# Query masking moved from GpSimd to VectorE, and the branch over a fallback program placed ahead of the last stores with prefetch hints

## The chip, the cores and the metric

The kernel runs on one core of one Trainium2 chip. The core has a matrix engine (TensorE, PE), a vector engine (VectorE, DVE), an activation engine (ScalarE, ACT), a general engine (GpSimd, POOL) and an engine that here only issues DMA transfers (SyncE, SP). They run their own instruction streams and wait for each other through semaphores. The metric is the device time of one launch in microseconds (us); lower is better.

## The reference

The input x has 2048 rows of 512 numbers in bfloat16. It is normalised once, and two branches read the result: an attention block with 32 heads of only 16 dimensions, and a gated feed-forward block of width 1792. Both are added to x.

```python
def _A_ref(x, wqkv, wo):          # H = 32, Dh = 16
    q, k, v = ...                 # (x @ wqkv) split in heads
    scores = jnp.einsum("bhqd,bhkd->bhqk", q, k) * (Dh ** -0.5)
    p = _softmax(scores, axis=-1)
    o = jnp.einsum("bhqk,bhkd->bhqd", p, v)
    return ... @ wo
def _B_ref(x, w1, w3, w2):
    h = _silu(x @ w1) * (x @ w3)
    return h @ w2
xn = _layernorm(x, axis=-1)
return x + _A_ref(xn, A_wqkv, A_wo) + _B_ref(xn, B_w1, B_w3, B_w2)
```

The exponentials are the bulk: 32 heads x 2048 x 2048 scores.

## The kernel before

**Units and chunks.** The attention is cut into 32 units. A unit is one block of 512 queries with four heads, which share the 128 partitions in four groups of 32 rows; each group of 32 holds two heads of 16 dimensions, and an even and an odd unit use one and the other of them. So the same projected queries serve two units (u0 and u0 + 1), once with the rows of the odd heads set to zero and once with the rows of the even heads set to zero. This is what the two masks `msk[:, 0:1]` and `msk[:, 1:2]` do. The tile `QT` has four slots of 128 x 512 for it. A chunk is a pair of score matmuls (L1794, two banks of PSUM, 128 x 1024 numbers); there are 1024 chunks, 32 for each unit, and three PSUM buffers for them.

**Two ways to an exponential.** A chunk goes either to ACT, which takes the exponential in one instruction (L1857, tile `PT`), or to DVE, which builds it from integer arithmetic: a first pass out of PSUM (`p1`, L1930) for each chunk, and then for every two chunks the four passes `m` (L1972), `g` (L1988), `t` (L1979) and `e` (L1994) within SBUF (tile `xd`). PE multiplies either result with the values (L2048).

**The planner.** The order of all instructions on all engines is made by a planner (`_Sched`), when the kernel is built. It plays the work through with a cost for each kind of instruction and gives every chunk to ACT or DVE as they come free; the rest of the work (projections, the feed-forward block, output projections) is put in between when its due position is reached or when PE has room. The due position is counted in score matmuls already issued (64 for a unit). What is on the chip is then a fixed order for each engine, with semaphore waits where data cross from one engine to another.

**The query projection.** `tile_QT(qc, i)` computes one block of projected queries for the unit pair u0, u0 + 1: sixteen matmuls on PE (L1331, with `wq`), then DVE takes the block out of PSUM with a scale (L1462) into slot s1. Then GpSimd makes the two masked copies in four instructions of 128 x 256 (L1470), each posted to start beside a `p1` of DVE (`beside_p1`, and the extra dependence on `st["p1_op"]`). There are 15 such tiles; the first pair of units gets its queries in another way. A tile is due 100 score matmuls before the first score that needs it (L1707). GpSimd's other recurring work is the product L2107 (`onorm`, two halves for each unit pair), which also starts beside a `p1`.

**The end.** After the last unit, PE, ACT and DVE finish four output tiles. They are stored by two DMA transfers of 256 KB that SP issues (L1636). The arithmetic on DVE is exact enough only within limits. DVE therefore checks these limits and writes a word `flag` (L2245); if it is set, a second, slower program (`_plan_max`) must run instead. `run` puts it on every engine: first the whole fast program, then a wait for the flag, a load of it into a register (L2304), and an `If` with the whole slow program inside (L2305 to L2313), which on these inputs is jumped over. SP then waits for its transfers (`emit_end`, L142), and all engines meet in a final barrier (L2316).

## Time and profile before

| what | us |
|---|---|
| time, median of 3 runs | 791.72 |
| lowest and highest of these runs | 790.52 and 792.25 |
| the profiled execution, its own time | 792.25 |
| its span in the trace | 790.5 |
| busy: ACT | 768.5 |
| busy: DVE | 763.5 |
| busy: PE | 747.2 |
| busy: POOL | 90.4 |
| ACT exponentials (L1857) | 796, busy 745.1 |
| DVE first passes `p1` (L1930) | 228, busy 277.2 |

A row of the profile gives line, engine, operation, the tile written and the tile read, the shapes, the count, and then the busy time with the mean duration of one instruction in nanoseconds. Consecutive instructions of an engine overlap a little in the records, so that the step from one start to the next is shorter than the duration: in an unbroken stretch of 90 exponentials it is 0.918 us where the mean duration is 1.161 us, and the passes L1972 and L1988 that follow each other at 35.82, 36.43 and 37.03 us step by 0.60 us where one lasts 0.685 us.

The own time of the profiled execution is 1.75 us more than its span: that part lies outside the first and the last recorded instruction.

### The profile page before, as it was taken

The numbers are of one execution on the slowest core, as the hardware profiler recorded it, in microseconds if no ns is written. First come the engines' busy times: TensorE is split into PE (matmuls) and PEld (weight loads), VectorE is DVE, ScalarE is ACT, GpSimd is POOL, SyncE is SP. The second block draws the span as 40 slices with busy tenths as digits, with TensorE's granted clock in tenths as the row PEclk, the third lists the DMA queues.
The fourth block names the chain that finished last, engine by engine and source line by source line (L and its number), as shares of the span: only waits on it lengthen the run. The fifth ranks groups of instructions, "written<-read, shape, count | busy, mean of one in ns | idle before, by whom it ended". The sixth has DMA issues, their size and how long they took to land.

```text
span 790.5 us, 21316 instructions
## 1 busy us (share of the span) xinstructions
PE 747.2 (95%) x9177; PEld 223.6 (28%) x9177; DVE 763.5 (97%) x1015; ACT 768.5 (97%) x870; POOL 90.4 (11%) x120
## 2 busy tenths in 40 slices
PE   8999999899999999989999999999899999999987
PEld 6422222222222222222222222222222222222223
DVE  8899999999999999999999999999999999999992
ACT  6999999999999999999999999999999999999993
POOL 3200012002020010302102020110201001020000
PEclk9999999999999999999999999999999999999998
DMA  7023122322232232333321134332122343132221
GB/s 214 2 23 114 9 36 29 49 30 32 52 41 22 36 38 36 46 47 49 50 14 33 25 56 49 49 42 28 37 22 22 62 56 37 35 48 16 29 14 34
DMA packets 83440, 32.92 MB, mean 42 GB/s; under 512 B 72072, under 2 KB 79496, under 8 KB 83336
## 3 DMA queue, kind: packets, MB, share of 16 engines
q1 hardware_dynamic: 83336, 31.46, 28.0%
q8 instruction: 74, 1.21, 0.6%
q14 instruction: 30, 0.25, 0.1%
HBM read 22.81 MB, written 2.10 MB: 32 GB/s over the span
## 4 chain that ended last, share of the span: by engine, by line
ACT 80%; PE 11%; DVE 8%; issue 1%; DMA 0%; POOL 0%; DVEq 0%; ACTq 0%
ACT f_PT L1857 76%; PE ps L1331 4%; PE ps L1794 3%; ACT f_th L1554 3%; DVE f_xd L1930 3%; PE ps L2048 2%; DVE f_xd L1979 1%; DVE f_xd L1994 1%; DVE f_xd L1988 1%; DVE f_xd L1972 1%; DVE f_hT L1568 0%; DVE f_t L1558 0%; DMA f_xd<-in_A_x_dram 0%; PE ps L1343 0%; DVE f_stats L1255 0%
## 5 line engine op out<-in xcount | busy, mean ns | idle before, releaser
L1857 ACT ACTIVATE f_PT<-ps 128x1024 bf16<-128x1024 f32 x796 | 745.1, 1161 | 3.8 <-PE ps L1794 3.6
L1794 PE MATMUL ps<-f_QT,f_KT 32*128 32x512 bf16 x2048 | 314.0, 385 | 25.1 <-ACT f_PT L1857 19.0
L1930 DVE TENSOR_SCALAR f_xd<-ps 128x1024 int16<-128x1024 f32 x228 | 277.2, 1216 | 2.3 <-PE ps L1794 1.8
L2048 PE MATMUL ps<-f_PT,f_Vaug 128*17 128x512 bf16 (+1 forms) x1592 | 202.8, 384 | 1.1 <-DVE f_U L2066 0.5
L2048 PE MATMUL ps<-f_xd,f_Vaug 128*32 128x512 bf16 (+1 forms) x1368 | 179.0, 384 | 5.5 <-DVE f_U L2066 3.8
L1794 PEld LDWEIGHTS ps<-f_QT,f_KT 32*128 32x128 bf16 x2048 | 80.2, 91 | 325.8 <-ACT f_PT L1857 265.2
L1331 PE MATMUL ps<-f_xnT,f_w 128*32 128x512 bf16 x1792 | 142.2, 384 | 3.7 <-DVE f_t L1558 1.8
L1979 DVE TENSOR_TENSOR f_xd<-f_xd 128x2048 bf16<-128x2048 bf16 x114 | 139.3, 1222 | 0.0
L1470 POOL TENSOR_SCALAR f_QT<-f_QT,f_msk 128x256 bf16<-128x256 bf16 x60 | 55.4, 923 | 271.7 <-DVE f_xd L1988 112.3
L1972 DVE TENSOR_SCALAR f_xd<-f_xd 128x2048 int16<-128x2048 int16 x114 | 78.0, 684 | 2.7 <-PE ps L2048 2.0
L1988 DVE TENSOR_SCALAR f_xd<-f_xd 128x2048 int16<-128x2048 int16 x114 | 78.1, 685 | 0.0
L1994 DVE TENSOR_SCALAR f_xd<-f_xd 128x2048 int16<-128x2048 int16 x114 | 78.1, 685 | 0.0
L1331 PE MATMUL ps<-f_w,f_hT 128*32 128x512 bf16 x896 | 72.6, 383 | 0.2 <-DVE f_xn_sb L1624 0.2
L2107 POOL TENSOR_TENSOR f_onorm<-f_U,f_R 128x256 bf16<-128x256 f32 x30 | 25.1, 845 | 371.8 <-DMA f_R<-f_Rrow 186.4
L2048 PEld LDWEIGHTS ps<-f_PT,f_Vaug 128*17 128x17 bf16 (+1 forms) x1592 | 49.4, 92 | 59.0 <-issue 45.0
L2048 PEld LDWEIGHTS ps<-f_xd,f_Vaug 128*32 128x32 bf16 (+1 forms) x1368 | 44.1, 92 | 48.9 <-issue 27.8
L1331 PEld LDWEIGHTS ps<-f_xnT,f_w 128*32 128x32 bf16 x1792 | 36.4, 94 | 64.5 <-issue 55.6
L1554 ACT ACTIVATE f_th<-ps 128x512 f32<-128x512 f32 x56 | 41.1, 733 | 0.0
L1568 DVE SCALAR_TENSOR_TENSOR f_hT<-f_t,ps 128x512 bf16<-128x512 bf16 x56 | 37.9, 677 | 0.3
L1558 DVE SCALAR_TENSOR_TENSOR f_t<-f_th,ps 128x512 bf16<-128x512 f32 x56 | 37.9, 677 | 0.2
L1331 PEld LDWEIGHTS ps<-f_w,f_hT 128*32 128x32 bf16 x896 | 19.4, 95 | 23.9 <-issue 16.8
L1331 PE MATMUL ps<-f_wo,f_onorm 128*32 128x512 bf16 x272 | 21.8, 408 | 0.2 <-DVE f_wkv L1613 0.2
(81 smaller groups left out, 244.2 us busy)
## 6 DMA issues: line engine op xcount, KB each, us to landing
f_w<-in_B_w_dram SPq DMA_DIRECT2D x112, 128.0 KB
f_R<-f_Rrow SPq DMA_DIRECT2D x124, 32.0 KB
f_xr<-in_A_x_dram SPq DMA_DIRECT2D x16, 128.0 KB
f_U<-f_U SPq DMA_DIRECT2D x60, 32.0 KB
f_w<-in_B_w_dram SPq DMA_DIRECT2D x7, 256.0 KB
f_xd<-in_A_x_dram SPq DMA_DIRECT2D x3, 512.0 KB
out_dram<-f_xn_sb SPq DMA_DIRECT2D x12, 128.0 KB
f_xd<-in_A_x_dram SPq DMA_DIRECT2D x2, 256.0 KB
```

Source lines behind the costliest of these rows:

```text
L1331: ins = e.matmul(bank(bk)[32 * i:32 * i + 32, 0:ncols], make_lhsT(i), rhs_ap, start=start, stop=stop, tile_position=(0, 32 * i))
L1470: q = P.op("pool", lambda e: e.tensor_scalar(QT[:, d_, cs], QT[:, s1, cs], msk[:, h:h + 1], None, ALU.mult), reads=[("QT", s1), ("msk", h) ...
L1554: q = P.op("act", lambda e: e.activation(th[:, ss, :], bank(bk), ACTF.Tanh, scale=0.5), reads=[("ps", bk)], writes=[("th", ss)], dur=a_cos ...
L1558: q2 = P.op("dve", lambda e: e.scalar_tensor_tensor(t1[:, ss, :], th[:, ss, :], 1.0, bank(bk), ALU.add, ALU.mult), reads=[("th", ss), ("ps ...
L1794: ins = e.matmul(bank(b), l_, r_, start=True, stop=True, tile_position=(rp, 0))
L1857: q = P.op("act", lambda e: e.activation(PT[:, s_, :], ps[:, b0 * 512:(b0 + 2) * 512], ACTF.Exp, scale=ASC, bias=ABIAS), reads=[("ps", b0) ...
L1930: q = P.op("dve", lambda e: e.tensor_scalar(dsl[:, ys, 1024 * c:1024 * c + 1024], ps[:, b0 * 512:b0 * 512 + 1024], YB, G_LO, ALU.add, ALU. ...
L1972: P.op("dve", lambda e: e.tensor_scalar(dsl[:, NY + m_, 0:n], y, 0x7F, 0x3F00, ALU.bitwise_and, ALU.bitwise_or), reads=YK, writes=[("ds", ...
L1979: q_ = P.op("dve", lambda e: e.tensor_tensor(t_ap.bitcast(BF16), y.bitcast(BF16), t_ap.bitcast(BF16), ALU.mult), reads=YK + [("ds", NY + m ...
L1988: q_ = P.op("dve", lambda e: e.tensor_scalar(g_ap, y, -G_LO, 0.0, ALU.add, ALU.max), reads=YK, writes=[("g", g_, k) for k in range(n // 51 ...
L1994: q_ = P.op("dve", lambda e: e.tensor_scalar(y, y, 0x7F80, None, ALU.bitwise_and), reads=YK, writes=YK, dur=s_cost(n), name="e", lock=True)
L2048: ins = e.matmul(bank(PV)[32 * j:32 * j + (17 if g % 2 == 0 else 32), :], v_, p_, start=s0, stop=s1, tile_position=(0, 32 * j))
```

## The change

There are two independent parts.

The masked copies leave GpSimd. DVE makes them right after the scaled copy out of PSUM, with two instructions of 128 x 512, the first from slot s1 to slot s0 and the second in place in s1. GpSimd keeps only its other product. The due position of a query tile goes from 100 to 60 score matmuls ahead. (The helper `beside_p1` moves to the place of its other user, unchanged.)

The fallback is left in another way. On every engine the code is now: the fast program up to a mark some 4 us before its end by the planner's clock, an instruction[...], the rest of the fast program, the load of the flag, and a compare-and-branch to one of two blocks. The slow block holds the slow program, the fast block only what is left. On SP the branch does not stand after all transfers, but before the first transfer that depends on something later than the flag: the two output transfers stand in both blocks, after the branch.

```diff
-    def emit_engine(self, e, handle, sems, dma_sems):
-        known = {}
-        for op in self.ops[e]:
+    def emit_engine(self, e, handle, sems, dma_sems, first=0, last=None, known=None):
+        known = dict(known or {})
+        for op in self.ops[e][first:last]:
...
+HINT_US = 4.0
...
-    QP_DUR = 0.5
...
             def emit():
                 q = P.op("dve", lambda e: e.tensor_scalar(QT[:, s1, :], bank(bk), QS, None, ALU.mult),
                          reads=[("ps", bk)], writes=[("QT", s1)], dur=d_cost(512), name="evQ")
                 rel(q)
-                P.post("pool", lambda: part(0), ready=q.end + _LAT, prio=1, cond=beside_p1)
-
-            def part(i):
-                h, cs = i // 2, slice(256 * (i % 2), 256 * (i % 2) + 256)
-                d_ = (s0, s1)[h]
-                q = P.op("pool", lambda e: e.tensor_scalar(QT[:, d_, cs], QT[:, s1, cs], msk[:, h:h + 1], None, ALU.mult),
-                         reads=[("QT", s1), ("msk", h)], writes=[("QT", d_)], dur=QP_DUR, name="evQ",
-                         extra=[st["p1_op"]])
-                if i % 2:
-                    done[("QTm", u0 + h)] = q.end + _LAT
-                if i < 3:
-                    P.post("pool", lambda: part(i + 1), ready=q.end + _LAT, prio=1, cond=beside_p1)
+                q = P.op("dve", lambda e: e.tensor_scalar(QT[:, s0, :], QT[:, s1, :], msk[:, 0:1], None, ALU.mult),
+                         reads=[("QT", s1), ("msk", 0)], writes=[("QT", s0)], dur=s_cost(512), name="evQ", lock=True)
+                done[("QTm", u0)] = q.end + _LAT
+                q = P.op("dve", lambda e: e.tensor_scalar(QT[:, s1, :], QT[:, s1, :], msk[:, 1:2], None, ALU.mult),
+                         reads=[("QT", s1), ("msk", 1)], writes=[("QT", s1)], dur=s_cost(512), name="evQ", lock=True)
+                done[("QTm", u0 + 1)] = q.end + _LAT
             P.post("dve", emit, ready=o.end + _LAT, prio=1)
...
-                crit.append((max(1, (qc * NG + 2 * i) * RPU - 100), k, tile_QT(qc, i)))
+                crit.append((max(1, (qc * NG + 2 * i) * RPU - 60), k, tile_QT(qc, i)))
...
+    ends = {k: len(PF.ops[k]) for k in _ENGS}
+    ends["sp"] = next(i for i, op in enumerate(PF.ops["sp"]) if op.deps and
+                      max(op.end for op in op.deps) > flag_op.end)
+
     def run(name, e):
-        PF.emit_engine(name, e, sems[0][0], sems[0][1])
+        ops = PF.ops[name]
+        n = ends[name]
+        mark = next(i for i in range(n) if ops[i].end > ops[n - 1].end - HINT_US or i == n - 1)
+        PF.emit_engine(name, e, sems[0][0], sems[0][1], 0, mark)
+        loc = e.mark_branch_hint_location()
+        PF.emit_engine(name, e, sems[0][0], sems[0][1], mark, n, PF.known)
+        known = PF.known
         e.wait_ge(sems[0][0]["dve"], flag_op.token[1])
         reg = e.alloc_register("slow_" + name)
         e.reg_load(reg, flag[0:1, 0:1])
-        with e.If(e.snap(reg) > 0):
+        e.br_cmp(reg, 0, on_true="fast_" + name, on_false="slow_" + name, comp_op="IS_LE").branch_hint(loc)
+        with nc.body("slow_" + name, valid_engines=[e.engine]):
+            PF.emit_engine(name, e, sems[0][0], sems[0][1], n, None, known)
             for k in _ENGS:
...
             PM.emit_end(name, e, sems[1][1])
-        PF.emit_end(name, e, sems[0][1])
+            e.br("end_" + name)
+        with nc.body("fast_" + name, valid_engines=[e.engine]):
+            PF.emit_engine(name, e, sems[0][0], sems[0][1], n, None, known)
+            PF.emit_end(name, e, sems[0][1])
+            e.br("end_" + name)
+        nc.switch_bb("end_" + name)
```

## The prediction

> **What bounds the kernel now.** I read the page first (sums, then costliest groups), then the table by stretches of time, then the chain that ended last in order of time, then the end of the trace line by line.
>
> ```profile
> PE 747.2 (95%) x9177; PEld 223.6 (28%) x9177; DVE 763.5 (97%) x1015; ACT 768.5 (97%) x870; POOL 90.4 (11%) x120
> ...
> L1857 ACT ACTIVATE f_PT<-ps 128x1024 bf16<-128x1024 f32 x796 | 745.1, 1161 | 3.8 <-PE ps L1794 3.6
> L1930 DVE TENSOR_SCALAR f_xd<-ps 128x1024 int16<-128x1024 f32 x228 | 277.2, 1216 | 2.3 <-PE ps L1794 1.8
> L1470 POOL TENSOR_SCALAR f_QT<-f_QT,f_msk 128x256 bf16<-128x256 bf16 x60 | 55.4, 923 | 271.7 <-DVE f_xd L1988 112.3
> ```
> ```profile
> 100.00:200.00 100.00, 94.55 (x1128) 26.39 (x1124) 99.69 (x129) 100.00 (x115) 13.19 (x16) 1.00 0.31 36
> 600.00:700.00 100.00, 96.12 (x1146) 26.84 (x1138) 99.37 (x128) 99.84 (x115) 11.01 (x14) 1.00 0.35 46
> 768.30:775.10 6.80, 6.34 (x56) 1.45 (x52) 3.56 (x5) 5.19 (x6) 0.00 (x0) 0.50 0.28 29
> ```
> ```profile
> 30.38 82.59 ACT f_PT L1857 x90
> ```
>
> In the stretches (busy PE, PEld, DVE, ACT, POOL, then granted clock, DMA share, GB/s) ACT is busy 100 of 100 us and DVE 99. The chain runs along ACT's exponentials; 90 of them take 82.59 us, 0.918 us each. So the middle is bound by ACT and DVE together: 796 + 228 chunks are shared out so that both end at once. GpSimd is idle nine tenths of the time, so what leaves it gives back nothing of itself. In the third row PE ran at half clock for 6.8 us, and ACT was busy only 5.19 of them; the timeline shows it idle 1.61 us before the exponential at 774.17.
>
> ```profile
> 785.49 0.69 DVE L1624 TENSOR_TENSOR f_xn_sb<-ps,f_wkv 128x512 bf16<-128x512 f32 x1 [1.09 <-PE ps L1331]
> 786.20 0.34 SPq L1636 DMA_DIRECT2D out_dram<-f_xn_sb  x1
> ...
> L2304 SPq TENSOR_LOAD <-flag x1: 511/511/511, 786.6 to 786.6; - x1
> ...
> L2305 PEldq COMPARE_BRANCH  x1: 4392/4392/4392, 784.4 to 784.4; - x1
> L2305 DVEq COMPARE_BRANCH  x1: 72/72/72, 786.2 to 786.2; - x1
> L2305 SPq COMPARE_BRANCH  x1: 55/55/55, 787.2 to 787.2; - x1
> ...
> L142 SPq EVENT_SEMAPHORE  x3: 28/28/28, 789.9 to 790.0; - x3
> ...
> L2316 DVEq DRAIN  x1: 57/57/57, 789.5 to 789.5; - x1
> L2316 SPq DRAIN  x1: 13/13/13, 790.3 to 790.3; - x1
> ```
>
> The last computed tile is ready at 786.18, the last store goes out at 786.20, and yet the span ends at 790.5. SP loads the flag at 786.60, branches at 787.24, and its next instruction (L142) starts at 789.90: 2.6 us without an instruction. DVE likewise branches at 786.16 and is next seen at 789.54. The packet records of the last store show 13 small closing packets at 787.70 to 787.85 and the last ones at 788.31 to 789.08, while instruction packets run on the same DMA engines.
>
> [...] 2.6 us on SP, 3.3 on DVE, and instruction packets there. [...] The trace has 684 ns at L1972[...]; but L1242, the only such instruction with operands read for each partition, takes 406 ns for 512 and steps by 0.32 us, more than a quarter of 0.60. [...] of 114 `t` passes (L1979) 7 lie over a GpSimd instruction by more than 0.1 us, mean 1.35 instead of 1.21 us.
>
> **The change part by part.** The compiled order of both kernels can be compared without running them, and it gives counts and neighbours.
>
> *Masks on DVE.* 30 instructions of 128 x 512 are new on DVE. By L1972's step (0.60 us for 2048[...]) one is 0.21 us, by L1242's step 0.32. That is 6.3 to 9.6 us on an engine without room. Against it the order has 226 `p1` instead of 228 and 113 of each further pass instead of 114: 2 x 1.13 + 3 x 0.60 + 1.13 = 5.2 us less. The two chunks are now ACT's: 798 exponentials, and 2 x 0.918 = +1.8 us on the path. One copy of values goes from DVE to ACT and one of transposed rows the other way (0.5 to 0.6 us each): zero in sum. The 60 GpSimd instructions were beside other work, so 0 gained; their contention, at most 7 x 0.13 us and four passes by 0.1 to 0.2, comes to 1.6 us on DVE together with L2107's, which stays; I take 0 on the path.
>
> *The due position.* In the order of before, the first query tile stands behind 28 score matmuls, with 100 more to go before its unit starts. In the new order it stands behind all 128 of the first two units, and the first score of the third unit waits for DVE with nothing of the earlier units left. So ACT must run dry there. From the start of the last old score to the next exponential: 0.3 us for that pair, 1.1 from the projection's start to its evacuation (27.30 to 28.41 in the trace of before), 0.6 for that (L1462's step), 0.2 to 0.3 for the first mask, perhaps 0.2 more for the second, 0.4 from a score to its exponential: 2.7 to 2.9. ACT still has one exponential (0.92) and part of the one before (0.4 to 0.5). Missing: about 1.5 us. Ends: 0.8 if two whole exponentials are in hand, 2.4 if DVE is still busy with an `e` and a copy of keys when the projection is done. The stall can't be made up later, as ACT has no idle time. For the other 14 tiles 24 to 60 score matmuls remain between projection and first use; at 2048 in about 760 us that is 9 to 22 us: covered.
>
> *The branch.* SP's flag load and branch now come before the stores. The flag is written at 782.67 to 782.82, plus 0.5 for the load and 0.2 to branch: 783.5, and the first store is due at 784.43. If the hint has the target there, SP issues the last store at the same moment as before, its closing packets come at 787.85 (the other engines' fetches are then over too), and from the last wait to the end it is 0.46 us (790.05 to 790.51)[...]: end at 788.4, -2.1. DVE's branch is at 786.2 and then costs nothing. If the hint does nothing, DVE's fetch still ends at 789.54 and only SP's last steps go: about -0.6. [...] I take -2.1, since the hint stands some 4 us ahead and a fetch took 2.6 to 3.3.
>
> *The tail* between the last exponential (777.6) and the last tile (786.2) has the same pieces; 44 matmuls instead of 48 follow the last product, about 0.2 us less, which I leave out.
>
> Sum: +1.8 + 1.5 - 2.1 = +1.2 us. Against the profiled execution's own time (792.25, span 790.5 and 1.75 around it): 793.5. That execution is 0.5 above the median of before, 791.72, and had a half-clock stretch in its tail, which other executions may not have had at that place; from the median it would be 792.9. I take 793.4, close to the first, since the masks are more likely above 0.21 us than below.
>
> **The rivals.**
> 1. The hint hides nothing: order alone gives -0.6 instead of -2.1, so 794.9. [...] Against: fetch time fits into the distance.
> 2. DVE falls behind: with masks at 0.32 us or more, 30 x 0.11 = 3.3 us come on top of what the order allows for. DVE was idle 0.3 to 1.6 us in each 100, which takes up about half; the rest holds PE, then ACT: 795.
> 3. Not slower: ACT doesn't run dry at the third unit, because PE finishes scores enough ahead of ACT that the three PSUM buffers cover the projection. Its place is the one spot near 65 us, its price the 1.5 us, and it decides as soon as two to three exponentials (1.84 to 2.75 us) are in hand when the projection starts. Then +1.8 - 2.1 from the median: 791.4. Against it: ACT frees a buffer before PE fills it, so rarely more than 1.5 are in hand. The half-clock stretch gone from the tail (1.6 us) would look the same in the sum.
> 4. The hint does harm: [...] 2.6 us instead of -2.1: 798.
>
> **How the numbers follow.** Chances: forecast 0.48, rival 1 0.18, rival 2 0.13, rival 3 0.17, rival 4 0.04. Predicted: 793.4. Range 791.2 to 795.7: the stall at either end (-0.7, +0.9), rival 3 below, rivals 1 and 2 above; rival 4 is left out. The forecast alone would be 792.3 to 794.6. This kernel's measurement tells 0.2% (1.6 us) from no change: below 790.1 is faster, above 793.3 slower. Over 793.3 lie about half of the forecast, nearly all of rivals 1, 2 and 4: 0.55. Below 790.1: the low end of rival 3, 0.07. Between: 0.38.
>
> **What would show it.** 798 exponentials with ACT still at 100 of 100 us from 100 us on; one idle gap of ACT of about 1.5 us before 70 us, released by PE, which waited for DVE's mask; masks between 290 and 410 ns in the records; from the last store's issue to the end of the span 2.2 us instead of 4.3, and no 2.6 us hole on SP. It would be wrong if the gap near 65 us is missing, if DVE's lateness makes idle time on ACT at every unit pair, or if holes of 2 us and more stand behind the branches as before.

## The result, and the profile after

| | before | after |
|---|---|---|
| median of 4 executions, us | 791.24 | 798.63 |
| lowest and highest | 790.52, 792.25 | 798.25, 799.01 |
| the profiled execution: own time, span | 792.25, 790.5 | 799.01, 797.3 |
| mean granted clock of TensorE, profiled execution | 0.995 | 0.993 |

The changed kernel takes 1.0093 times as long (95% interval 1.0075 to 1.0110), 7.4 us more. Forecast were 793.4 us and a range of 791.2 to 795.7, so the measured time lies above the range.

First the page of the changed kernel: the sums, and the groups of the exponentials and of the first passes. (The lines of code have other numbers than before: L1794 is now L1785, L1857 is L1848, L1930 is L1921, L1636 is L1627.)

```profile
PE 751.4 (94%) x9169; PEld 227.9 (29%) x9169; DVE 768.8 (96%) x1039; ACT 772.0 (97%) x872; POOL 37.6 (5%) x60
...
L1848 ACT ACTIVATE f_PT<-ps 128x1024 bf16<-128x1024 f32 x798 | 748.0, 1144 | 5.7 <-PE ps L1785 5.0
...
L1921 DVE TENSOR_SCALAR f_xd<-ps 128x1024 int16<-128x1024 f32 x226 | 274.7, 1215 | 3.0 <-PE ps L1785 2.7
```

Two exponentials more, two first passes fewer, GpSimd down from 90.4 to 37.6 us: the counts are those forecast. ACT's idle time before its exponentials went from 3.8 to 5.7 us, so part of the loss is not in their number. The table of groups by shape has DVE's copy out of PSUM and the two masks (count, busy, mean ns, idle before):

```profile
L1459 DVE TENSOR_SCALAR f_QT<-ps 128x512 bf16<-128x512 f32 x15 | 10.2, 678 | 0.7 <-PE ps L1331 0.7
L1462 DVE TENSOR_SCALAR f_QT<-f_QT,f_msk 128x512 bf16<-128x512 bf16 x15 | 5.3, 353 | 0.5
L1465 DVE TENSOR_SCALAR f_QT<-f_QT,f_msk 128x512 bf16<-128x512 bf16 x15 | 5.2, 347 | 0.0
```

The masks last 350 ns; from one start to the next they take 0.269 and 0.263 us. The copy now steps by 0.717 us instead of 0.60; the instruction behind it now reads its result. Copy and masks together take 1.25 us of DVE for each tile, where the planner reckons with 1.015.

Next the place near 66 us: the chain of waits in that stretch, in order of time (start, duration, what), and after it the lines of the timeline (PE's matmuls between the copy and the next score, that score, and the exponential behind it).

```profile
66.07 0.39 PE ps L1785 x2
66.46 1.01 PE ps L1331 x16
...
67.49 0.70 DVE f_QT L1459
68.19 0.03 issue
68.22 0.35 DVE f_QT L1462
```
```profile
68.24 0.51 PE L1506 MATMUL ps<-f_wkv,f_xnT 128*32 128x384 bf16 x8
68.68 0.60 PE L1785 MATMUL ps<-f_QT,f_KT 32*128 32x512 bf16 x6
69.15 1.02 ACT L1848 ACTIVATE f_PT<-ps 128x1024 bf16<-128x1024 f32 x1 [1.30 <-PE ps L1785]
```

The last score of the old units, then the projection, its copy and the first mask, and ACT without work for 1.30 us in the records (from start to start it is 1.66 us more than the usual step of an exponential). This is the dry place of the forecast, at its size.

Then the table by stretches (busy PE, PEld, DVE, ACT, POOL, granted clock, DMA share, GB/s) for the 3.4 us ahead of the half-clock stretch in the tail, and the stretch itself:

```profile
764.85:768.25 3.40, 2.23 (x18) 0.59 (x18) 3.37 (x4) 3.40 (x5) 0.00 (x0) 1.00 0.12 13
768.30:778.50 10.20, 10.07 (x66) 2.42 (x66) 9.77 (x13) 8.66 (x10) 0.00 (x0) 0.50 0.35 24
```

PE runs at half clock for 10.2 us, against 6.8 before, and fills them; ACT works only 8.66 of them. In the 3.4 us ahead of it PE was busy 2.23 us, with 18 matmuls. In the profiled execution of before the place ahead of its stretch was sparse too:

```profile
764.90:768.30 3.40, 2.45 (x24) 0.60 (x20) 3.40 (x5) 3.40 (x5) 0.00 (x0) 1.00 0.61 24
```

Last the end: the answers for the lines of the hint (the instruction of `mark_branch_hint_location` stands in the trace as BRANCH_PREFETCH_HINT and takes 36 to 56 ns), the flag's load, the branch, the stores, the waits for them and the barrier (durations min/median/max in ns, first and last start in us).

```profile
L2303 SPq BRANCH_PREFETCH_HINT  x1: 56/56/56, 769.1 to 769.1; - x1
...
L2303 DVEq BRANCH_PREFETCH_HINT  x1: 51/51/51, 787.3 to 787.3; - x1
...
L2308 SPq TENSOR_LOAD <-flag x1: 475/475/475, 789.3 to 789.3; - x1
...
L2309 SPq COMPARE_BRANCH  x1: 75/75/75, 789.8 to 789.8; - x1
...
L2309 PEldq COMPARE_BRANCH  x1: 1339/1339/1339, 790.5 to 790.5; - x1
L2309 DVEq COMPARE_BRANCH  x1: 84/84/84, 792.3 to 792.3; - x1
...
L1627 SPq DMA_DIRECT2D out_dram<-f_xn_sb x2: 408/891/1374, 792.8 to 793.2; - x2
...
L142 SPq EVENT_SEMAPHORE  x3: 28/28/28, 794.7 to 796.8; - x3
...
L2327 DVEq DRAIN  x1: 58/58/58, 796.2 to 796.2; - x1
```

The holes stand behind the branches as before: SP branches at 789.8 and issues its first store at 792.8, DVE branches at 792.3 and is next seen at 796.2. The last tile is ready at 792.38, so SP's hole, which lay behind the last store, now lies ahead of both. They go out bunched, and the last tile to the end of the span takes 4.89 us; before it was 4.34.

**The sum of the two profiled executions.** ACT's undisturbed step from start to start is 0.904 us for an exponential and 0.477 us for a gate activation (`f_th`). What a step has beyond that is excess. By this count, the 6.8 us of the two profiled executions come from:

| part | before | after | difference |
|---|---|---|---|
| first exponential starts at | 11.84 | 12.48 | +0.64 |
| undisturbed work of ACT (796 and 798 exponentials) | 749.3 | 751.1 | +1.8 |
| excess up to 70 us | 2.35 | 3.95 | +1.60 |
| excess in the middle, up to some 760 us | 10.40 | 12.29 | +1.89 |
| excess in the last 20 us before the last exponential ends | 2.70 | 2.89 | +0.19 |
| last exponential to last tile | 9.59 | 9.65 | +0.06 |
| last tile to the end of the span | 4.34 | 4.89 | +0.55 |

The first row scatters from 11.8 to 12.5 us over all kernels with the same beginning, so I don't count it as a cost of the change. Both profiled executions have a half-clock stretch in the last 20 us, so the table shows next to nothing of its price. Of the middle's 1.89 us, 1.2 are in the steps from a gate activation to the exponential behind it (56 of them, 0.43 us in all before, 1.65 after).

**The clock.** Each execution comes with its mean granted clock. The 147 executions of the kernel before that ran beside the experiments can be put in order by it (three clocks with one or three executions each are left out):

| mean clock | executions | median us |
|---|---|---|
| 1.000 | 37 | 790.3 |
| 0.999 | 8 | 790.0 |
| 0.998 | 34 | 791.0 |
| 0.996 | 33 | 792.2 |
| 0.995 | 21 | 792.4 |
| 0.992 | 7 | 793.6 |

A straight line through all of them gives 0.46 us for each 0.001 and 790.2 us at full clock, with a scatter of 0.5 us around it. The half-clock stretches in the traces last 3.41 us or a multiple (3.41, 6.83, 10.24); one of 3.41 takes 0.5 x 3.41 / 790 = 0.0022 off the mean, about 1.0 us. The four executions of the changed kernel stand at 0.992 to 0.993, the median of before at 0.998. Below, "at full clock" is a time less 0.46 us for each 0.001 that its clock is below 1: an estimate from this line. It is rough to some 0.5 us, as the mean also counts half clock behind the last matmul, which delays nothing (in the profiled execution of before 1.7 us of it, 0.0011 of the missing 0.0054). For the changed kernel it is 795.2 us, 5.0 more than before; by this estimate 2.4 us of the 7.4 are clock.

### The profile page after: what moved, and what is told of

It is laid out like the page before. It is cut to its first block, busy times and chain, and to the rows that moved or that the text cites. A ratio compares the mean times of both kernels' runs of the same rounds, so it can differ in the third digit from the quotient of the medians.

```text
span 797.3 us, 21182 instructions
## 1 busy us (share of the span) xinstructions
PE 751.4 (94%) x9169; PEld 227.9 (29%) x9169; DVE 768.8 (96%) x1039; ACT 772.0 (97%) x872; POOL 37.6 (5%) x60
## 4 chain that ended last, share of the span: by engine, by line
ACT 70%; DVE 19%; PE 9%; issue 1%; DVEq 0%; ACTq 0%
ACT f_PT L1848 67%; DVE f_xd L1921 7%; PE ps L1331 3%; DVE f_xd L1970 3%; PE ps L1785 3%; ACT f_th L1545 2%; DVE f_xd L1963 2%; PE ps L2039 2%; DVE f_xd L1979 2%; DVE f_xd L1985 2%; DVE f_hT L1559 1%; DVE f_t L1549 1%; PE ps L1218 1%; DVE f_U L2057 1%; DVE f_QT L1459 0%
## 5 line engine op out<-in xcount | busy, mean ns | idle before, releaser
L1848 ACT ACTIVATE f_PT<-ps 128x1024 bf16<-128x1024 f32 x798 | 748.0, 1144 | 5.7 <-PE ps L1785 5.0
L1785 PE MATMUL ps<-f_QT,f_KT 32*128 32x512 bf16 x2048 | 310.7, 386 | 27.3 <-ACT f_PT L1848 21.3
L1921 DVE TENSOR_SCALAR f_xd<-ps 128x1024 int16<-128x1024 f32 x226 | 274.7, 1215 | 3.0 <-PE ps L1785 2.7
L2039 PE MATMUL ps<-f_PT,f_Vaug 128*17 128x512 bf16 (+1 forms) x1596 | 210.2, 385 | 3.6 <-DVE f_U L2057 2.1
L2039 PE MATMUL ps<-f_xd,f_Vaug 128*32 128x512 bf16 (+1 forms) x1356 | 182.7, 385 | 3.7 <-DVE f_xd L1970 1.6
L1785 PEld LDWEIGHTS ps<-f_QT,f_KT 32*128 32x128 bf16 x2048 | 79.6, 91 | 323.5 <-ACT f_PT L1848 259.6
L1331 PE MATMUL ps<-f_xnT,f_w 128*32 128x512 bf16 x1792 | 139.9, 384 | 2.7 <-DVE f_t L1549 1.2
L1970 DVE TENSOR_TENSOR f_xd<-f_xd 128x2048 bf16<-128x2048 bf16 x113 | 137.1, 1213 | 0.0
L1331 PE MATMUL ps<-f_w,f_hT 128*32 128x512 bf16 x896 | 74.5, 388 | 0.2
L2057 DVE COPY f_U<-ps 128x512 f32<-128x512 f32 x31 | 21.2, 683 | 0.4 <-PE ps L2039 0.4
L1331 PE MATMUL ps<-f_wo,f_onorm 128*32 128x512 bf16 x272 | 20.0, 382 | 0.2 <-DVE f_QT L1459 0.2
```

The lines of the kernel that those rows point to most:

```text
L1331: ins = e.matmul(bank(bk)[32 * i:32 * i + 32, 0:ncols], make_lhsT(i), rhs_ap, start=start, stop=stop, tile_position=(0, 32 * i))
L1785: ins = e.matmul(bank(b), l_, r_, start=True, stop=True, tile_position=(rp, 0))
L1848: q = P.op("act", lambda e: e.activation(PT[:, s_, :], ps[:, b0 * 512:(b0 + 2) * 512], ACTF.Exp, scale=ASC, bias=ABIAS), reads=[("ps", b0) ...
L1921: q = P.op("dve", lambda e: e.tensor_scalar(dsl[:, ys, 1024 * c:1024 * c + 1024], ps[:, b0 * 512:b0 * 512 + 1024], YB, G_LO, ALU.add, ALU. ...
L1970: q_ = P.op("dve", lambda e: e.tensor_tensor(t_ap.bitcast(BF16), y.bitcast(BF16), t_ap.bitcast(BF16), ALU.mult), reads=YK + [("ds", NY + m ...
L2039: ins = e.matmul(bank(PV)[32 * j:32 * j + (17 if g % 2 == 0 else 32), :], v_, p_, start=s0, stop=s1, tile_position=(0, 32 * j))
```

## The experiments

Each time is a median; the ratio (with its 95% interval) is to the kernel before, run beside it. The first row is the median of all 147.

| run | us | ratio | median clock | at full clock |
|---|---|---|---|---|
| (before) | 791.4 | | 0.998 | 790.2 |
| (changed kernel) | 798.63 | 1.0093 (1.0075 to 1.0110) | 0.993 | 795.2 |
| e1_masks | 797.46 | 1.0077 (1.0053 to 1.0102) | 0.995 | 794.9 |
| e2_branch | 790.24 | 0.9988 (0.9977 to 0.9999) | 0.9985 | 789.7 |
| e3_masks_due100 | 793.79 | 1.0029 (1.0018 to 1.0040) | 0.998 | 792.2 |
| e5_masks_costs | 795.78 | 1.0046 (1.0028 to 1.0064) | 0.998 | 794.1 |
| e6_early_hint | 790.39 | 0.9997 (0.9984 to 1.0010) | 0.998 | 789.9 |
| e7_no_hint | 791.22 | 1.0003 (0.9993 to 1.0012) | 0.997 | 789.9 |
| e9_masks_small | 798.00 | 1.0088 (1.0064 to 1.0113) | 0.992 | 794.3 |
| e10_slow_first | 799.63 | 1.0107 (1.0089 to 1.0126) | 0.9925 | 796.4 |
| e11_jump_early | 790.89 | 0.9991 (0.9981 to 1.0002) | 0.997 | 789.5 |
| e12_masks_jump_early | 796.26 | 1.0076 (1.0051 to 1.0100) | 0.996 | 794.2 |
| e14_due108 | 794.00 | 1.0036 (1.0025 to 1.0047) | 0.998 | 793.4 |
| e15_masks_due70 | 799.17 | 1.0100 (1.0071 to 1.0129) | 0.9925 | 796.2 |
| e16_changed_filled | 796.71 | 1.0068 (1.0049 to 1.0087) | 0.9985 | 796.1 |
| e17_before_filled | 791.99 | 1.0006 (0.9998 to 1.0014) | 0.999 | 791.6 |
| e18_jump_filled | 791.30 | 0.9995 (0.9983 to 1.0006) | 0.999 | 790.8 |
| e19_changed_filled_other | 800.60 | 1.0118 (1.0093 to 1.0143) | 0.9925 | 797.4 |
| e20_jump_filled_short | 790.68 | 0.9989 (0.9980 to 0.9998) | 0.998 | 789.8 |
| e21_due100_jump | 792.39 | 1.0011 (0.9999 to 1.0023) | 0.998 | 791.5 |

### The two parts alone, and the due position

The masks with the due position of 60, and the ending of before:

```diff
-            e.br_cmp(reg, 0, on_true="fast_" + name, on_false="slow_" + name, comp_op="IS_LE").branch_hint(loc)
+            with e.If(e.snap(reg) > 0):
```

> The kernel before with the masks on DVE and the due position 60, and the old ending. Theory M (the masks and their due position carry nearly all of the loss): last exponential about 6 us later than before, span from last DVE tile to the end 4.3 us as before, time about 797.4. Theory B (the new ending carries most): last exponential at most 3.3 us later, time 793 to 794.5.

The ending alone, in the kernel before:

```diff
-            with e.If(e.snap(reg) > 0):
+            e.br_cmp(reg, 0, on_true="fast_" + name, on_false="slow_" + name, comp_op="IS_LE").branch_hint(loc)
```

> The kernel before with only the new ending. Theory M: last exponential as before, 4.9 us instead of 4.3 from the last DVE tile to the end, since SP stands still 2.9 us behind its branch while the tiles are done; time 791.2 + 0.6 = 791.8. Theory B: the hint takes fetches from PE or DVE in the tail, holes of 2 us and more there, time 795 or more. If the hint did what I forecast: 789.1.

The masks with the old ending and the old due position:

```diff
-                crit.append((max(1, (qc * NG + 2 * i) * RPU - 60), k, tile_QT(qc, i)))
+                crit.append((max(1, (qc * NG + 2 * i) * RPU - 100), k, tile_QT(qc, i)))
```

> e1 with the due position back at 100. If the idle gap of ACT near 66 us comes from the due position: no gap there, about 2 us less than e1, 795.4. If it comes from the masks on DVE themselves: the gap stays, time as e1.

Measured: 797.46, 790.24 and 793.79 us. The loss is nearly all in the first part. The ending alone is 0.9 us below before, and not above it as its first theory had: in that trace SP's hole ends 0.27 us ahead of the last tile. With a due position of 100 the loss is 2.0 us at full clock: the two exponentials (798, and no step over 0.4 us near 66 us). With 60 it is 4.7 us, and the clock goes from 0.998 to 0.995. The trace of the masks with 60 has the same step of 1.66 us excess at 66.0 us and 13.9 us of excess in the middle, one half-clock stretch of 3.41 us at 311 us among it; another, of 6.83 us, is in the tail. The due position of 60 with the masks still on GpSimd was not run.

The same masks with due position 100, and the planner told what the three DVE instructions take:

```diff
-                         reads=[("ps", bk)], writes=[("QT", s1)], dur=d_cost(512), name="evQ")
+                         reads=[("ps", bk)], writes=[("QT", s1)], dur=0.717, name="evQ")
...
-                         reads=[("QT", s1), ("msk", 0)], writes=[("QT", s0)], dur=s_cost(512), name="evQ", lock=True)
+                         reads=[("QT", s1), ("msk", 0)], writes=[("QT", s0)], dur=0.269, name="evQ", lock=True)
```

> e3 with the planner told what the masks cost in the trace (0.717, 0.269 and 0.263 us for evacuation and masks instead of 0.597, 0.209 and 0.209). If the slow loss of some 2 us over the middle is lateness against the plan (0.23 us for each of 15 tiles, 3.5 us): the planner moves one or two more chunks to ACT and the waits go, 1 to 2 us less than e3, about 794. If it isn't: as e3 or 1 us more.

795.78 us: another order, 799 exponentials, and 1.9 us slower at full clock than with the wrong costs. The expectation of about 794 us missed: true costs don't make a better order here.

### Is DVE late?

```diff
-                    q = P.op("dve", lambda e: e.tensor_scalar(QT[:, s0, :], QT[:, s1, :], msk[:, 0:1], None, ALU.mult),
+                    q = P.op("dve", lambda e: e.tensor_scalar(QT[:, s0, 0:64], QT[:, s1, 0:64], msk[:, 0:1], None, ALU.mult),
...
-                    q = P.op("dve", lambda e: e.tensor_scalar(QT[:, s1, :], QT[:, s1, :], msk[:, 1:2], None, ALU.mult),
+                    q = P.op("dve", lambda e: e.tensor_scalar(QT[:, s1, 0:64], QT[:, s1, 0:64], msk[:, 1:2], None, ALU.mult),
```

> Masks on VectorE and due position 60 with the old ending, with the same order of instructions, but each mask instruction treats 64 of the 512 columns and the other columns of the masked copies are zero from the start, once: so seven eighths of the masking is left out and the output isn't the reference's. Each mask is then some 0.15 to 0.2 us shorter. Theory 1 (VectorE falls behind its plan, since evacuation and masks take 1.25 us for each tile where the plan has 1.015, and this makes the small waits of ScalarE in the middle): 797.5 falls by 2 to 4 us to 793.5 to 795.5, with the middle's sum of excess steps from 13.9 down to 10 to 11 us, and the gap at 66 us shortened by 0.2 to 0.4. Theory 2 (the waits come from the order itself, where PE's work stands between the score matmuls): at most the 0.2 to 0.4 us of the gap go, 797.0 to 797.4, and the middle's sum stays near 13.

Two of the four slots of `QT` are set to zero once at the start (not shown in the diff). The groups of the two masks in this run:

```profile
L1463 DVE TENSOR_SCALAR f_QT<-f_QT,f_msk 128x64 bf16<-128x64 bf16 x15 | 3.6, 241 | 0.5
L1466 DVE TENSOR_SCALAR f_QT<-f_QT,f_msk 128x64 bf16<-128x64 bf16 x15 | 3.5, 235 | 0.0
```

From start to start they take 0.152 and 0.146 us, so that copy and masks come to 1.02 us for a tile: DVE keeps to its plan, and 3.5 us of lateness over the 15 tiles are gone. The order is the same. The time is 798.0 us, above both theories, as the clock was at 0.992; at full clock it is 0.6 us less than with whole masks, and the excess in the middle is 11.5 us (12.3 in the changed kernel, which like this run has no half-clock stretch there). The gap at 66 us keeps its 1.66 us: PE issues eight matmuls of the value projection (L1506) between the copy and the next score, which cover the mask, long or short. The theory of a late DVE falls as the main cause: its share is about that 0.6 us, and four executions of each don't tell it well.

### Does a later due position cost in proportion, and what does another order cost?

```diff
-                crit.append((max(1, (qc * NG + 2 * i) * RPU - 60), k, tile_QT(qc, i)))
+                crit.append((max(1, (qc * NG + 2 * i) * RPU - 70), k, tile_QT(qc, i)))
```

> Masks on VectorE with the old ending and a due position of 70 score matmuls. In this order the first query tile stands 20 score matmuls ahead of the unit that needs it (0 with 60, 100 with 100), all others about 60 ahead. Theory 1 (what the due position of 60 costs is the one place near 66 us where ScalarE runs dry, plus what the order does to the middle by chance): no gap there, the sum of excess steps before 70 us back from 4.0 to 2.5, and 793.5 to 795.5. Theory 2 (a later due position costs in proportion, at all tiles): 796 to 797.5, with the middle's sum at 13 to 14.

```diff
-                crit.append((max(1, (qc * NG + 2 * i) * RPU - 100), k, tile_QT(qc, i)))
+                crit.append((max(1, (qc * NG + 2 * i) * RPU - 108), k, tile_QT(qc, i)))
```

> The kernel before with masks on GpSimd and its old ending, and a due position of 108 instead of 100: no part of the change, only another order of the same instructions. Theory 1 (another order alone moves the time by a us or two, since the small waits of ScalarE in the middle and the number of exponentials it gets depend on it): the middle's sum of excess steps moves from 10.4 to 11.5 or more, or the number of exponentials by one or two, and the time by 1 us or more, mostly up. Theory 2 (the order as such is neutral, and only what is named, exponentials and a dry place, counts): 796 exponentials, 10.0 to 10.8, and 790.5 to 791.7.

With 70 the gap is gone (excess up to 70 us 2.37), as the first theory had it, but the time is 799.2: 799 exponentials, 15.7 us of excess in the middle (a half-clock stretch of 6.83 us at 121 us among it), and executions with clocks from 0.988 to 1.000. The only one of them at full clock took 795.4. So neither theory's number held; the price there is the order and the clock. With 108 and the masks on GpSimd, no part of the change, it is 794.0 us with the clock of before. Most of this order's loss lies behind the last exponential, where its chain of waits has

```profile
781.06 6.62 PE ps L1331 x120
787.71 0.69 DVE f_xn_sb L1624
```

120 matmuls of output projections, where before has 64 in 3.60 us at this place: from the last exponential to the last tile it is 12.6 us instead of 9.6. So another order of the very same instructions cost 3 us here; none of the orders tried was better than that of before.

### The ending

The hint 150 us ahead, and no hint at all, both in the kernel before with the new ending:

```diff
-HINT_US = 4.0
+HINT_US = 150.0
```

> The kernel before with the new ending only, and the hint 150 us ahead of the branch instead of 4 (by the planner's clock). Theory 1 (the hint works, but 4 us or the place behind the last long wait is too late): the holes of 2.5 us on SP and 3.5 us on DVE behind their branches close, instruction packets are seen soon after the hints, and the time falls from 790.2 (new ending with the hint 4 us ahead) to 788.0 to 788.8. Theory 2 (the hint of these engines fetches nothing, wherever it stands): holes as with 4 us, no packets behind the hints, 790.0 to 790.5. Theory 3[...]: packets soon after the hints, and holes nevertheless; 790.2.

```diff
-            loc = e.mark_branch_hint_location()
...
-            e.br_cmp(reg, 0, on_true="fast_" + name, on_false="slow_" + name, comp_op="IS_LE").branch_hint(loc)
+            e.br_cmp(reg, 0, on_true="fast_" + name, on_false="slow_" + name, comp_op="IS_LE")
```

> The kernel before with the new ending, without any hint. Theory 1 (the 0.9 us that the new ending gains come from the order alone: the branch of SP ahead of the stores): 790.2, and the same holes of 2.5 us on SP and 3.5 us on DVE. Theory 2 (the hint helps PE at least, whose branch took 0.5 us instead of 4.4, and so the end): 790.6 to 791.1, with PE's branch back at 4 us. Theory 3 (the hint does harm): 789.5.

At full clock the three are 789.7 (4 us), 789.9 (150 us) and 789.9 (none): 0.3 to 0.5 us less than before, and no difference between them that can be told. In the traces there is one. Without a hint PE's branch takes 3739 ns, with either hint 0.5 us (in the changed kernel's order 1.3 us, in the lines above). SP's and DVE's holes are 2.7 and 3.1 us without a hint and 2.5 and 3.5 with the hint at 4 us, but with the hint at 150 us (lines of the branch, the stores, the waits and the barrier):

```profile
L2316 SPq COMPARE_BRANCH  x1: 75/75/75, 782.3 to 782.3; - x1
...
L2316 DVEq COMPARE_BRANCH  x1: 84/84/84, 785.0 to 785.0; - x1
...
L1637 SPq DMA_DIRECT2D out_dram<-f_xn_sb x2: 337/343/349, 783.3 to 785.1; - x2
...
L142 SPq EVENT_SEMAPHORE  x3: 28/28/28, 785.5 to 788.2; - x3
...
L2334 DVEq DRAIN  x1: 52/52/52, 785.6 to 785.6; - x1
```

DVE goes on 0.6 us after its branch, and SP issues the last store at 785.1, as soon as the tile is ready. So on SP, DVE and ACT the holes close with the early hint, as the first theory had it. But it missed twice. No instruction packet of their own is seen behind the hints: from 600 to 660 us, where four of them stand (627 to 634 us), the trace has eight instruction packets, and the trace without any hint has the same eight. How the early hint closes the holes stays open. And the gain did not come: the last store still lands 3.1 us after its issue. The DMA view of that stretch shows who shares the DMA engines with it:

```profile
q1 hardware_dynamic: 288, 0.52, 28.7%
q14 instruction: 3, 0.02, 2.3%
q8 instruction: 1, 0.02, 2.0%
```

Four instruction packets of 8 and 16 KB run beside the 256 KB store. An ending without any shows the difference:

```diff
+            PF.emit_engine(name, e, sems[0][0], sems[0][1], 0, h)
+            e.br("fast_" + name)
+            with nc.body("slow_" + name, valid_engines=[e.engine]):
...
+            with nc.body("fast_" + name, valid_engines=[e.engine]):
+                PF.emit_engine(name, e, sems[0][0], sems[0][1], h, None, known)
...
+                e.br_cmp(reg, 0, on_true="end_" + name, on_false="slow_" + name, comp_op="IS_LE")
+            nc.switch_bb("end_" + name)
```

> The kernel before with masks on GpSimd, and the slow program laid in the stream behind each engine's first few instructions, where it is jumped over while loads are awaited; at the end the flag decides between a far branch back (slow) and falling through to the end, which lies right behind. Theory 1 (the end costs a fetch of code that lies far away, 2.5 to 3.5 us, and nothing else hides it): no hole behind the branches, the last tile to the end of the span 2.0 to 2.5 us instead of 4.3, the start not later by more than 0.5 us, so 788.5 to 789.5. Theory 2 (what is awaited at the end is the landing of the last stores, and the fetch lies beside it): 790.2 to 791. Theory 3 (the jump at the start costs its own fetch on the path): the first exponential 2 to 3 us later, 791 to 792.5.

The end is as expected: last tile to the end of the span 2.54 us, the last store issued at 795.7 and landed at 797.8, 2.0 us. The DMA view of the last 5 us has the stores alone:

```profile
q1 hardware_dynamic: 288, 0.52, 27.9%
issues: line engine op xcount, KB each, median us to landing
```

But the jump at the start costs 11.7 us, four times what the third theory had: the timeline there has

```profile
3.67 0.69 DVE L1255 BATCH_NORM_STATS2 f_stats<-f_xd 128x6 f32<-128x512 bf16 x1 [0.40 <-DMA f_xd<-in_A_x_dram]
8.93 0.69 DVE L1255 BATCH_NORM_STATS2 f_stats<-f_xd 128x6 f32<-128x512 bf16 x1 [4.57 <-issue]
```

and SP, which issues the loads, stands for 5.2 us too; ACT stands for 2.6 us, GpSimd not at all. Why DVE and SP stand longer here than behind their branches at the end (2.5 to 3.9 us) was not shown. PE stands for 1.96 us too, and its granted clock is 0.70 in the first 20 us and 0.99 in the next 80, against 1.00 in before: 13.7 us more at half clock. So the jump went to where each engine waits anyway, shortly before its end:

```diff
+        cut = {"dve": PF.ops["dve"].index(flag_op) - 7, "act": len(PF.ops["act"]) - 1,
+               "pool": len(PF.ops["pool"]), "sp": len(PF.ops["sp"]) - 2}
...
+            PF.emit_engine(name, e, sems[0][0], sems[0][1], 0, cut[name])
+            e.br("last_" + name)
```

> The kernel before with masks on GpSimd, and another ending: on ACT, DVE, SP and GpSimd the slow program is laid in the stream ahead of the last few instructions, behind the point where each engine has a long wait shortly before its end (ACT and DVE some 6 us, SP 17 us, GpSimd 30 us), and is jumped over there; at the end the flag decides between a far branch back and falling through to the end. PE keeps a far branch with a hint. Theory 1 (the fetch behind the branch is what the end waits for, and it can be hidden only where an engine waits anyway): the last tile to the end of the span 2.4 to 2.7 us instead of 4.3, no hole on SP or DVE after the last tile, nothing lost in the start: 789.0 to 789.7. Theory 2 (part of the fetch returns at the end, as the code of the end is again in another block): 790.2 to 790.8. Theory 3 (the jump comes too late for DVE or ACT and delays their last work): 791 to 793, with the last exponential to the last tile longer than 9.6 us.

790.89 us, at full clock 0.7 us less than before. There is no hole and no loss, but the end takes 3.69 us, not 2.5: one instruction packet, 1.8 us long, runs beside the last store, which lands after 3.2 us (PE still has a far branch here; whether the packet is for it was not shown):

```profile
q1 hardware_dynamic: 288, 0.52, 23.3%
q8 instruction: 1, 0.02, 1.9%
```

So the time is above the first two ranges. In the 20 traces the last store lands 2.9 to 3.6 us after its issue wherever an instruction packet runs beside it, and 2.0 us in the one trace without; one packet of 1.3 to 1.8 us goes with 2.9 to 3.3 us. That the packet is the cause fits all of them, though only one trace has none. That PE's branch too can be placed so wasn't tried.

The same ending in the changed kernel, and with the due position of 100 besides:

> The changed kernel (masks on VectorE, due position 60) with the ending of the early jump in place of its own. Theory 1 (of the 7.4 us by which the changed kernel is slower, the ending with its fetch ahead of the stores has a part, as SP's hole of 2.9 us ends only after the last tile is ready and both stores go out bunched): the last tile to the end of the span 2.5 instead of 4.9 us, 796.0 to 796.6. Theory 2 (the ending has no part in it, and the difference of the changed kernel to the one with the old ending is scatter): 797.3 to 798.6.

```diff
-                    crit.append((max(1, (qc * NG + 2 * i) * RPU - 60), k, tile_QT(qc, i)))
+                    crit.append((max(1, (qc * NG + 2 * i) * RPU - 100), k, tile_QT(qc, i)))
```

> Masks on VectorE with a due position of 100 and the ending of the early jump: the changed kernel with both repairs. Theory 1 (the parts add up: two exponentials 1.8 us, and the early jump's gain of 0.7): mean clock 0.997 to 0.999 as in before, 792.3 to 793.2. Theory 2 (the ending in the order of the masks gains more, as it did with due position 60, 2.4 us): 791.2 to 792.

796.26 us: last tile to end 3.35 instead of 4.89 us, 1.0 us less at full clock, so the changed kernel's own ending may have a part (five executions against four). The other 1.4 us to 798.63 are clock (0.996 instead of 0.993), which this run doesn't explain. With due position 100 too it is 792.39 us, 1.3 more than before at full clock: what is left are the two exponentials less the ending's gain, as the first theory had it. This is the changed kernel with its due position and its ending replaced; it does not gain on before.

### The clock

The stretches of one trace begin and end on one grid of 3.41 us, which lies elsewhere in each execution (counted from the span's start in steps of 3.413 us, a stretch begins 0.3 us after a step in before, 0.9 with the early hint and 1.5 with due position 70). Cut into the windows of this grid, the fourteen traces that have stretches between the start and the last matmuls show sixteen of them. The window ahead of each is among the three of its execution (some 220) with the least work of PE, counted as the sum of its matmuls' durations (6.5 to 9.2 us, as matmuls overlap in the records). But 29 windows with no more than 9.2 us have no stretch behind them, so the limit isn't known. Why executions of the same kernel stand at clocks from 0.992 to 1.000 was not shown. By the table of stretches, of the kernel with due position 70 and then of the kernel with the early hint:

```profile
117.60:121.00 3.40, 2.35 (x24) 0.72 (x24) 3.40 (x6) 3.40 (x6) 0.00 (x0) 1.00 0.00 0
121.00:127.80 6.80, 6.80 (x50) 1.15 (x48) 6.38 (x9) 5.17 (x7) 0.00 (x0) 0.50 0.12 24
```
```profile
304.70:308.10 3.40, 2.52 (x22) 0.66 (x14) 3.40 (x6) 3.40 (x6) 0.00 (x0) 1.00 0.00 0
308.10:311.50 3.40, 3.20 (x30) 1.01 (x30) 2.55 (x4) 2.89 (x4) 0.00 (x0) 0.50 0.15 30
```

The middle of before has 93 to 98 us of PE's 100 busy and some 38 matmuls in each 3.4 us. The test fills just the sparse place at 757 to 772 us, by issuing each score there twice in the same order:

```diff
-                for (b, l_, r_, rp) in mms:
-                    ins = e.matmul(bank(b), l_, r_, start=True, stop=True, tile_position=(rp, 0))
+                for k in range(2 if 994 <= n < 1013 else 1):
+                    for (b, l_, r_, rp) in mms:
+                        ins = e.matmul(bank(b), l_, r_, start=True, stop=True, tile_position=(rp, 0))
```

> The changed kernel, in which the score matmuls of chunks 994 to 1012 (PE at about 757 to 772 us, the sparse place ahead of and in the half-clock stretch) are each issued twice; nothing else differs, the order neither. Theory 1 (the half-clock stretch comes where PE had little work in a window of 3.4 us): it is gone or shorter in the tail, the mean clock rises from 0.9925 to 0.996 or more, and the time falls from 798.6 to 795.5 to 797. Theory 2 (the stretch is chance, or has another cause): the clock stays at 0.992 to 0.994 and the time at 798 to 799.5, since the doubled matmuls cost a little.

The same with chunks 940 to 958, at a dense place:

```diff
-                for k in range(2 if 994 <= n < 1013 else 1):
+                for k in range(2 if 940 <= n < 959 else 1):
```

> The changed kernel with the score matmuls of chunks 940 to 958 (PE at about 717 to 731 us, where PE is dense) issued twice. Theory 1 (only the sparse place counts): clock 0.992 to 0.993 and the tail's stretch as in the changed kernel, time 798.5 to 800. Theory 2 (more work of PE anywhere near the end keeps the clock up): the clock rises and the time falls as where the sparse place is filled.

796.71 against 800.60 us. The same places in the two traces, filled and filled elsewhere:

```profile
764.60:768.00 3.40, 3.10 (x36) 0.67 (x29) 3.33 (x5) 3.39 (x5) 0.00 (x0) 1.00 0.08 6
768.00:778.20 10.20, 9.59 (x102) 2.79 (x102) 9.67 (x13) 10.20 (x12) 0.00 (x0) 1.00 0.37 26
```
```profile
766.45:769.85 3.40, 2.16 (x18) 0.58 (x16) 3.37 (x4) 3.40 (x5) 0.00 (x0) 1.00 0.13 9
769.90:780.10 10.20, 10.18 (x68) 2.43 (x68) 9.63 (x13) 8.55 (x9) 0.00 (x0) 0.50 0.35 25
```

With 36 instead of 18 matmuls ahead of it the stretch is gone, ACT is busy for all of the 10.2 us, and all four executions stand at 0.998 to 1.000. Filled elsewhere, the stretch is there with its 10.24 us, and the time is 2.0 us above the changed kernel: the price of 19 doubled pairs. So the sparse place makes the half clock. At full clock 19 doubled pairs cost 0.9 us at the sparse place and 2.2 at the dense one, so without them the clock would give back more than the 1.9 us seen. ACT's excess in the last 20 us is of the same size as the 2.4 us taken from the clocks: 2.9 us in the changed kernel, 0.5 with the place filled, and 0.3 in the early jump, whose trace has no stretch.

In the kernel before and in the early jump with 17 doubled pairs, and in the early jump with six:

```diff
+                for k in range(2 if 1003 <= n < 1020 else 1):
```

> The kernel before, in which the score matmuls of chunks 1003 to 1019 (PE at about 757 to 771 us) are each issued twice. Theory 1 (a sparse window of PE brings the half clock): the stretch near 768 us, which some executions of before have, is gone, the mean clock is 0.998 to 1.000 in nearly all of them, and the time falls from 791.2 to 790.2 to 790.7. Theory 2 (chance): clocks spread from 0.992 to 1.000 as before, 791 to 792.

> The early jump over the slow program (masks on GpSimd) together with the doubled score matmuls of chunks 1003 to 1019. Theory 1 (both gains are real and add up): 789.2 to 790.0, about 1.5 us less than before. Theory 2 (only the ending counts): 790.7 to 791.

```diff
-                for k in range(2 if 1003 <= n < 1020 else 1):
+                for k in range(2 if 1011 <= n < 1017 else 1):
```

> The kernel before with the early jump and only six doubled pairs of score matmuls, chunks 1011 to 1016 (PE at about 763 to 768 us). Theory 1 (what brings the half clock is the one window ahead of it, and six pairs fill it; each doubled pair costs some 0.08 us, as 17 cost 1.3): mean clock 0.998 to 1.000, 789.8 to 790.4, less than before and than the early jump alone. Theory 2 (six are too few, or fall into the wrong window): clocks from 0.993 to 1.000 as with the jump alone, 791 to 791.5.

17 pairs raise the clock (no execution of 32 below 0.997) and cost what they give, 1.3 to 1.4 us at full clock: 791.99 and 791.30 us, so that both expectations of a gain missed. Six pairs cost 0.3 us, keep all 21 executions at 0.997 or above, and come to 790.68 us, 0.9989 of before, above the 789.8 to 790.4 expected. That and the new ending alone (0.9988) are the only versions whose interval lies below 1; both gain 0.8 to 0.9 us, half of what a measurement of this kernel tells from no change.

## Why the prediction was wrong

- **Masks on DVE, +1.8: right.** 798 exponentials; with the due position left at 100 the loss at full clock is 2.0 us. The masks' price, 0.263 to 0.269 us, lies between the bounds of 0.21 and 0.32 (the lower one was my estimate; the planner reckons with 0.209). The copy ahead of them was put at 0.6 us and takes 0.717, which the prediction missed. Rival 2 (DVE falls behind) had the lateness about right, 3.5 us over the 15 tiles, but not what it costs: with that lateness taken away 0.6 us are saved at full clock. What DVE loses beside GpSimd was small, as taken: the `t` passes last 1213 ns on average instead of 1222.
- **The dry place near 65 us, +1.5: right.** 1.66 us of excess at 66.6 us, gone with a due position of 70 or 100. Of its pieces, the 0.4 to 0.5 us put down to the masks belong to the eight matmuls of the value projection beside them; that these last as long is luck. Rival 3 is out. (The pieces as listed add up to 2.6 to 2.9 us, and the stall's two ends give 792.7 to 794.3 rather than 792.3 to 794.6; nothing rests on either.)
- **"For the other 14 tiles ... covered": right for that wait, but taken for more than it says.** In the trace PE waits for a mask once, 0.3 us at the first tile. The middle has 1 to 1.9 us more of small waits all the same, since the whole order is another one. The experiments with other due positions show such effects, up to 3 us and in other places; I had costed the new order at nothing but what the moved instructions do. Where it comes from within the order isn't settled, apart from the 1.2 us behind the gate activations and some 0.6 us of DVE's lateness.
- **The branch, -2.1: wrong; rival 1's reading is the right one.** The step "fetch time fits into the distance" failed: a distance longer than the holes of 2.6 to 3.3 us in before isn't enough. SP's hint stood 20.7 us ahead and its hole was still 2.9 us; with the hints 150 us ahead SP and DVE go on within 1.0 us of their branches. What decides between them stays open. In the order of before the new ending is worth -0.5 us, close to rival 1's -0.6; in the changed kernel +0.2 (795.2 against 794.9 at full clock, less than these can tell), where SP's hole ends 0.4 us after the last tile and the stores go out together. Also wrong was "SP issues the last store at the same moment as before ... end at 788.4" (0.1 us of it my estimate): the last store lands 3.1 us after its issue beside instruction packets, against 2.0 without them, so that the closed holes of the early hint gain nothing.
- **"The tail ... has the same pieces": wrong in the largest point.** I saw the half-clock stretch before, took it for a disturbance of that one execution, and put its cost at nothing. It follows from sparse work of PE, which the new order has at 765 us (2.23 us busy, 18 matmuls, in the profiled one). By the clocks of the four executions this cost 2.4 us more than in before (an estimate).
- **Rival 4** (the hint does harm) was not seen: no new wait on issue in PE's or DVE's tail. That its 798 us are the number nearest to the measured 798.63 is chance.

The sum in place of +1.2: +2.0 (exponentials) + 1.7 (dry place) + 1.0 (small waits) + 0.2 (ending) + 2.4 (clock) = 7.3 us, of the 7.4 measured. The third term is what is left of 4.7 - 2.0 at full clock after the gap, and the fifth is an estimate, so that the sum comes out is in part by construction.

## What to carry to other kernels

Where a planner makes the order, a change of a due position is a new order: look in it for places where the last of the old work is issued before the new operands are ready, and for windows where TensorE has little to do, and price both; here the first cost 1.7 us and the second brought the half clock for 3.4 to 10.2 us. Put each execution's time beside its granted clock before comparing versions; here six executions of one program spread over 0.9% with clocks from 0.988 to 1.000. Don't count on a hint for a far branch without a trace: 5 to 20 us ahead it closed no hole on SP, DVE or ACT here, and 150 us ahead it closed them and saved no time. Near the end of a program look also for instruction packets beside the last stores; the end was shortest, 2.5 us instead of 4.3, where the final code lay in one piece with what runs before it.

## What was not expected of the hardware

- A half-clock stretch of TensorE came behind windows of 3.4 us in which it was busy 2.1 to 2.8 us with 18 to 30 matmuls and, in before and after, never idle for more than 0.53 us (1.0 us at most in all sixteen). Doubling the matmuls of that window (18 to 36) removed it.
- With the branch hint PE's branch took 0.5 us instead of 3.7 already with the hint 5 us ahead (1.2 to 1.6 us in the orders with the masks on DVE). On SP, DVE and ACT the holes closed with the hint 150 us ahead but not 5 to 20 us ahead, and on GpSimd with neither (2.5 us until its next instruction). No instruction packet was seen behind the early hints that the kernel without hints doesn't have.
- With a single 16 KB instruction packet of 1.8 us beside it a 256 KB store landed 3.2 us after its issue; without any it was 2.0 us.
- `tensor_scalar` with an operand read for each partition, bfloat16, took 347 to 353 ns for 128 x 512 and still 235 to 241 ns for 128 x 64. From start to start it was 0.266 and 0.149 us on average, so that by an estimate from these two sizes some 0.13 us of each don't depend on the length.
- After a jump at the program's start, while the inputs are loaded, DVE stood still for 4.6 us, and the first exponential came 11.7 us later than in before.
